# Opening transfers planned with other lengths, new block ranks, and the first 128 keys in one load by ScalarE

## The chip, the cores and the metric

The kernel runs on one core of one Trainium2 chip. The metric is device microseconds of one execution; the kernel before takes 880.31 us (median of 3 runs, 880.14 to 880.77).

## What is computed

Three layers follow one another. First, attention with a sliding window of 64 keys on 4 sequences of 576 tokens, 8 heads of 64:

```python
scores = scale * np.matmul(q, k.transpose(0, 1, 3, 2))
mask = (rel >= 0) & (rel < window)
attn = softmax(np.where(mask, scores, -1e9)); attn_out = np.matmul(attn, v)
```

Its 2304 x 512 result goes through a gated layer (weights 512 x 1536 twice and 1536 x 512) and then through a second one (512 x 2048, 2048 x 512):

```python
xn = x / sqrt(mean(x*x) + 1e-6) * rms_g
y  = (silu(xn @ w_gate) * (xn @ w_val)) @ w_out
h  = y @ w_in;  out = (np.maximum(h, 0) ** 2) @ w_out2
```

Weights arrive as 8-byte numbers and are turned into a high and a low part on the chip ("decode").

## The kernel before

One function lists the work as steps: an engine (or two that may do it), a planned length, the tiles read and written, a rank, and a lag, the planned time from a step's end until its result can be used. `Schedule.issue` then lays all steps out against these planned lengths, always taking on the engine that is free first the step of lowest rank that is ready, and emits the instructions in that order. Each engine runs its own list in that order, and waits where an input is late. The lists are SP (SyncE, which issues nearly all transfers), PE, DVE, ACT, POOL. Where the plan leaves PE without work early on, it puts in matmuls on a constant tile (L1270, "filler").

Attention is cut into 36 blocks of 64 queries, n = 0, 1, 2, ... in the order of the list BLOCK. The order of sequences starts with blocks 0 and 1 of each sequence. For a block: load q (L461), keys (L437) and values (L465); scores on PE (L484); mask and row minimum on DVE (L489); exponentials on ACT (L491); transposes on PE (L500); copy of these by ACT or DVE (L258, tile pt); product with the values on PE (L510); division on DVE (L515); squares on ACT or DVE (L520, L522). Four or six blocks make a tile; per tile a matmul sums the squares (L535), DVE and POOL make the factor (L536, L537), DVE scales (L551), PE transposes (L556), ACT or DVE writes the high part (L258, R<-ps) and DVE the low part (L259, R<-ps).

With a tile's rows and decoded weights the gated layer's products run on PE (L660, L662, L664: "up" with R as input, "down" with ah, al or L). The decode of a pair of weights is: two loads into Q (L591), one scaling by ACT (L605) or DVE (L607), two casts by ACT (L610, L611), two steps by DVE (L612, L613), an addition (L614), then the split into parts (L258 R<-Q, L259 R<-Q). PE's up and down products fill the gaps between attention steps, by rank.

From about 157 us on, five groups of the rest of the first layer run; their upper products (L1116) read quarter sums of the tokens (xq), fetched by SP (L1091) into two slots in turn: a fetch can start when the product two before it has ended. In between SP also writes decoded weights of the second layer to scratch (L768, su and sd). From about 520 us the second layer runs (L883, L959).

Two helpers are named later: `attention(blocks, rank)` and `rms(t, rank, part)` make the steps above with a rank from `rank_at`, to which the lists BLOCK_RANK and NORM_RANK add an offset each.

Of the kernel before, what the change touches and what calls it, by code (L numbers as in the profile page):

```python
# [9 lines left out]
F32 = mybir.dt.float32  # L10
# [33 lines left out]
KW = 4  # L44
GROUPS = [2, 2, 2, 2, 2]
W0 = 9
QTILE, QRANK = 4, 68.0
BLOCK_RANK = [-9.1, 12.7, 56.1, -1.2, -48.4, -18.4, -13.1, -3.7, -7.9, 5.6, 2.2, 2.0, 3.1, 4.8, 3.7, -10.1, 1.4, 2.5, -2.8, -5.7]
NORM_RANK = [-15.0, -1.0, 11.2, 13.4, 14.7, 8.7, 2.9, -0.5]
FIRSTW = [-900.0, -14.0, -5.0]  # L50
CUT, VLATE = 1, 2.3
A1, A2 = 4, 4
S1, S2 = 2, 2
ZONE = 2 * UN
# [5 lines left out]
PG = 2  # L60
G32 = 32
SINGLE = 4
LEAD = 22.6
ELEAD = 13.7
FILL = 1.6, 9.0, 0.45
PORT, SHARED, OPENING = 1.0, 1.5, 0.3

# [180 lines left out]
def attn_moe_moe2(ctx: ExitStack, tc: tile.TileContext, qT, kT, vw, w1, w2, w3, w4, rms_g, out):  # L248
# [8 lines left out]
    nc = tc.nc  # L257
# [3 lines left out]
    sc = Schedule()  # L261
# [18 lines left out]
    T = Tiles()  # L280
# [92 lines left out]
    def at(*a, **k):  # L373
        attn_steps.append(sc.add(*a, **k))
# [7 lines left out]
    def setup():  # L382
        def build_mask():
            nc.gpsimd.memset(T["mask"], 0.0)

            for j in range(2):
                m = T["mask"][64 * j : 64 * j + 64, :]
                nc.gpsimd.affine_select(out=m, in_=m, compare_op=ALU.is_gt, fill=NEG, base=0, pattern=[[1, P]], channel_multiplier=-1)
                nc.gpsimd.affine_select(out=m, in_=m, compare_op=ALU.is_ge, fill=NEG, base=64, pattern=[[-1, P]], channel_multiplier=1)

        def build_ident():
            nc.gpsimd.memset(T["ident"], 1.0)
            nc.gpsimd.affine_select(out=T["ident"], in_=T["ident"], compare_op=ALU.is_equal, fill=0.0, base=0, pattern=[[-1, P]], channel_multiplier=1)
# [12 lines left out]

        at("pool", 0.3, build_expo, w=["expo"])
        at("pool", 1.0, build_comb, w=["comb"])
        at("act", 0.7, lambda: nc.scalar.dma_start(out=T["g"], in_=rms_g), w=["g"], lag=2.5, rank=-1001.0)
        g0 = NBLK - 4  # L410
        gb = T["acc"][:, :, g0 * WIN : (g0 + 1) * WIN]
        at("dve", 0.33, lambda: nc.vector.tensor_scalar(gb, T["g"].unsqueeze(2).to_broadcast([P, KC, WIN]), DM**0.5, None, op0=ALU.mult), r=["g"], w=allk("acc", (g0, 1)))
        gp = ps[R_BANK].rearrange("p (i r) -> p i r", i=NP)[:, :2]

        def spread_g():

            for h in range(2):
# [9 lines left out]
    def load_keys(b, i, rank):  # L427

        w0, w1 = max(i - 1, 0), KEYS[i]
        off = 2 * (b % 2) if i == 0 else 0  # L430
        k = k_tile[0][0] if off else k_ring.next()
        k_tile[0] = k, off - w0
        cuts = (0, 1, 2) if b == i == 0 else (w0, w1)
        for c0, c1 in zip(cuts, cuts[1:]):
            d = slice((c0 + off - w0) * WIN, (c1 + off - w0) * WIN)
            queue = "act" if b == i == c0 == 0 else "sp"
            at("sp", 0.2 + (c1 - c0) * WIN / 105, lambda c0=c0, c1=c1, d=d, queue=queue: (nc.scalar if queue == "act" else nc.sync).dma_start(out=T[k][:, :, d], in_=kT[b, :, :, c0 * WIN : c1 * WIN]), w=[(k, c) for c in range(c0 + off - w0, c1 + off - w0)], lag=2.0, rank=rank + c0 - 0.6 if i == 0 and b < 2 else None)  # L437

    def attention(blocks, rank):

# [10 lines left out]
    def block(n, rank, part, pos):  # L451

        b, i = BLOCK[n]
        nk = WIN if i == 0 else 2 * WIN
        early = lambda late: rank + late if n < T1[0][1] else None
        q, sm, pt = (r.next() for r in (q_ring, sm_ring, pt_ring))
        if i != 1:
            v_tile[0] = v_ring.next()
        v = v_tile[0]
        nb, su, rs = (small[i].next() for i in ("nb", "sum", "rs"))  # L460
        at("sp", 0.6, lambda: nc.sync.dma_start(out=T[q], in_=qT[b * NB + i]), w=[q], lag=2.0, rank=early(-0.5))  # L461
        if i in KEYS:
            load_keys(b, i, rank)
        if i != 1:
            at("sp", 0.75, lambda: nc.sync.dma_start(out=T[v], in_=vw[b * NB + i]), w=[v], lag=2.0, rank=early(VLATE))  # L465
        k, k0 = k_tile[0]
        k0 = (max(i - 1, 0) + k0) * WIN
        keys_ = T[k][:, :, k0 : k0 + nk]
# [108 lines left out]
    closed, closed2 = [], []  # L577
    early = iter(FIRSTW)

    def decode(srcs, rank=None, after=()):  # L580

        n = len(srcs) * WE
# [5 lines left out]
            raws, da, df = [f"raw{h}"], f"da{h}", f"{df_ring.slots[0]}{h}"  # L588
            raw = raws[0]
        for z, src in zip(raws, srcs):  # L590
            sc.add("sp", 2.4 if closed2 else 1.5, lambda z=z, src=src: nc.sync.dma_start(out=T[z], in_=src), w=[z], lag=2.2, rank=rank, after=after)  # L591
        part = lambda i: T[raw].rearrange("p (a b) -> p a b", b=2)[:, :, i]
        a = lambda: T[da]
        f = lambda: T[df]
# [163 lines left out]
    def park(src, keys_, n, dst, key):  # L758

        g = stage_ring.next()  # L760
        v = lambda i=slice(0, 2): T[g][:, : 2 * n].rearrange("p (h n) -> p h n", h=2)[:, i]

        def like(x):
            return x.rearrange("p (i m) -> p i m", m=256) if len(src().shape) == 3 else x

        sc.add(AD, c_ad(n), lambda e: copy(e, like(v(0)), src()), r=keys_, w=[g], port=True)
        sc.add(DP, c_dp(n), lambda e: two(e, like(v(1)), src(), like(v(0)).bitcast(F32), ALU.subtract), r=keys_ + [g], w=[g], port=True)
        sc.add("sp", 0.8 if n == 256 else 1.6, lambda: nc.sync.dma_start(out=dst, in_=v().bitcast(F32)), r=[g], w=[key], lag=2.5)  # L768

    def park_pair(z, p, srcs, swap):  # L770
        f = decode(srcs, after=closed2)
# [246 lines left out]
    QUADS = (B11, B21, R2, R3, R4, R1, B22)  # L1018
# [158 lines left out]
    n = 0  # L1177
    while n < NBLK:
        k = FIRST[max(i for i, t in enumerate(T1) if t[0] <= n)]
# [3 lines left out]
        n = e  # L1183
# [12 lines left out]
    todo, n = [], 0  # L1196
# [317 lines left out]
```

## Time and profile before

| | us |
|---|---|
| median of 3 runs | 880.31 |
| profiled execution | 879.84 |
| its span, first to last instruction | 878.1 |
| PE busy | 866.8 |
| DVE busy | 713.4 |
| ACT busy | 585.3 |

A row of the timeline gives the start, the length, the engine, the line, what is written <- read, and how many instructions it merges; in brackets stands the idle time of the engine before it and what ended it. A window's row gives the busy time and count of each engine, the granted TensorE clock and the share of the transfer engines. "PE" is the matmuls, "PEld" the weight loads beside them; one matmul of the program on 128 x 128 fp32 tiles with a constant as input is recorded as two.

### The profile page before, as it was taken

The page shows a single profiled execution, that of the slowest core. Times are in us where ns is not written, and L with a number is a line of the kernel's source. Part 1 is how long each engine was busy: PE and PEld are TensorE (multiplying, and loading weights), DVE is VectorE, ACT ScalarE, POOL GpSimd, SP SyncE. Part 2 cuts the span into 40 slices and gives each one's busy share as a digit, 9 for nine tenths or more (in the row PEclk, how much of TensorE's full clock was granted, in tenths as well). Part 3 has the DMA queues.
Part 4 walks back from the last instruction along what each step waited for, and adds up shares of the span by engine and source line. Part 5 has one row for each costly group of instructions (what it writes and reads, how often), then busy time and mean ns, then how long its engine had stood idle before and what let it go on. Part 6 is the DMA issues. An engine that isn't in the chain of part 4 may idle for free.

```text
span 878.1 us, 15620 instructions
## 1 busy us (share of the span) xinstructions
PE 866.8 (99%) x5766; PEld 810.5 (92%) x5766; DVE 713.4 (81%) x1407; ACT 585.3 (67%) x1194; POOL 129.3 (15%) x139
## 2 busy tenths in 40 slices
PE   8999999999999999999999999999999999999998
PEld 6789999989889889879989889999999999999997
DVE  5899997887897888898898877678885788767695
ACT  6999885666796786777677676546645546565360
POOL 4545550000040030040022000000100002000010
PEclk9999999999999999999999999999999999999999
DMA  8696782277777968768778698887779776788762
GB/s 262 198 293 220 253 301 89 97 276 253 263 288 267 322 225 299 265 241 299 256 262 266 227 311 293 302 295 264 249 261 305 265 252 238 259 289 290 254 205 72
DMA packets 88059, 222.26 MB, mean 253 GB/s; under 512 B 8240, under 2 KB 30256, under 8 KB 83504
## 3 DMA queue, kind: packets, MB, share of 16 engines
q1 hardware_dynamic: 86304, 220.46, 72.8%
q10 hardware_dynamic: 1680, 0.82, 0.3%
q8 instruction: 45, 0.74, 0.3%
q14 instruction: 30, 0.25, 0.1%
HBM read 179.83 MB, written 41.42 MB: 252 GB/s over the span
## 4 chain that ended last, share of the span: by engine, by line
PE 88%; DVE 6%; ACT 4%; issue 1%; DMA 0%; ACTq 0%; DVEq 0%
PE ps L883 20%; PE ps L959 19%; PE ps L660 12%; PE ps L662 11%; PE ps L664 11%; PE ps L1116 11%; ACT sm L491 2%; PE ps L484 1%; PE ps L500 1%; PE ps L510 1%; DVE sm L489 1%; ACT acc L491 1%; DVE R L259 1%; DVE Q L260 1%; DVE R L260 1%
## 5 line engine op out<-in xcount | busy, mean ns | idle before, releaser
L883 PE MATMUL ps<-R 128*128 128x384 f32 x1008 | 180.6, 334 | 0.0
L883 PEld LDWEIGHTS ps<-R 128*128 128x128 f32 x1008 | 175.4, 188 | 0.3
L959 PE MATMUL ps<-R,L 128*128 128x384 f32 x462 | 155.0, 336 | 0.0
L258 ACT COPY acc<-ps 128x384 f32<-128x384 f32 (+2 forms) x131 | 65.4, 501 | 57.5 <-PE ps L664 29.9
L1116 PE MATMUL ps<-R 128*128 128x512 f32 x420 | 101.8, 390 | 0.0
L1116 PEld LDWEIGHTS ps<-R 128*128 128x128 f32 x420 | 78.7, 188 | 15.8
L967 DVE TENSOR_TENSOR acc<-ps,acc 128x384 f32<-128x384 f32 x101 | 55.4, 555 | 40.9 <-PE ps L959 40.9
L959 PEld LDWEIGHTS ps<-R,L 128*128 128x128 f32 x462 | 86.6, 187 | 0.0
L660 PE MATMUL ps<-R 128*128 128x384 f32 (+2 forms) x368 | 79.9, 339 | 0.6 <-DVE s L713 0.6
L662 PE MATMUL ps<-R 128*128 128x384 f32 (+2 forms) x368 | 78.0, 333 | 0.0
L664 PE MATMUL ps<-R 128*128 128x384 f32 (+2 forms) x368 | 77.8, 333 | 0.0
L959 PE MATMUL ps<-L,R 128*128 128x384 f32 x220 | 74.1, 337 | 0.2 <-DVE acc L967 0.2
L660 PEld LDWEIGHTS ps<-R 128*128 128x128 f32 x368 | 61.9, 189 | 5.5 <-DVE s L713 0.9
L662 PEld LDWEIGHTS ps<-R 128*128 128x128 f32 x368 | 62.4, 188 | 3.2
L664 PEld LDWEIGHTS ps<-R 128*128 128x128 f32 x368 | 62.2, 189 | 3.2
L660 PE MATMUL ps<-L,R 128*128 128x512 f32 (+1 forms) x200 | 57.5, 368 | 0.5 <-ACT ps L742 0.5
L742 ACT COPY ps<-acc 128x512 f32<-128x512 f32 (+1 forms) x97 | 52.8, 554 | 7.7 <-DVE acc L258 5.4
L258 ACT CAST L<-Q 128x512 fp32r<-128x512 f32 (+2 forms) x80 | 44.1, 559 | 20.1 <-DVE Q L710 11.5
L662 PE MATMUL ps<-L,R 128*128 128x512 f32 (+1 forms) x200 | 57.4, 368 | 0.0
L664 PE MATMUL ps<-L,R 128*128 128x512 f32 (+1 forms) x200 | 57.4, 368 | 0.0
L931 ACT CAST L<-Q 128x1152 fp32r<-128x1152 f32 (+1 forms) x22 | 22.0, 998 | 50.1 <-PE ps L959 44.9
L959 PE MATMUL ps<-X,R 128*128 128x384 f32 x154 | 51.1, 332 | 0.0
(153 smaller groups left out, 1826.2 us busy)
## 6 DMA issues: line engine op xcount, KB each, us to landing
R<-xq SPq DMA_DIRECT2D x35, 1024.0 KB, 6.0
Q<-w SPq DMA_DIRECT2D x68, 512.0 KB, 4.7
R<-su SPq DMA_DIRECT2D x24, 1024.0 KB, 5.9
R<-su SPq DMA_DIRECT2D x24, 768.0 KB, 6.1
R<-sd SPq DMA_DIRECT2D x13, 1024.0 KB, 5.7
su<-L SPq DMA_DIRECT2D x24, 512.0 KB, 3.8
sd<-L SPq DMA_DIRECT2D x24, 512.0 KB, 5.2
L<-sd SPq DMA_DIRECT2D x11, 1024.0 KB, 7.7
```

Of the source, the lines that this page charges most:

```text
L258: copy = lambda e, out, in_: nc.scalar.copy(out, in_) if e == "act" else nc.vector.tensor_copy(out, in_)
L260: two = lambda e, out, a, b, op: (nc.vector if e == "dve" else nc.gpsimd).tensor_tensor(out, a, b, op=op)
L491: at("act", 0.37, lambda p=p: nc.scalar.activation(T[sm][:, p, :nk], T[sm][:, p, :nk], AF.Exp, bias=T[nb][:, p : p + 1], scale=-1.0, accum ...
L660: nc.tensor.matmul(acc, wh, xh, start=(i == 0 and not seeded), stop=False, skip_group_check=seeded)
L662: nc.tensor.matmul(acc, wl, xh, start=False, stop=False, skip_group_check=seeded)
L664: nc.tensor.matmul(acc, wh, xl, start=False, stop=(i == n - 1), skip_group_check=seeded)
L742: add("act", c_act(n), lambda b=b, dst=dst: nc.scalar.copy(ps[b][:, :n], dst), r=keys("acc", c, t), w=[("ps", b)])
L883: nc.tensor.matmul(bank, w_, x_, start=(start and i == 0), stop=(i == len(terms) - 1), skip_group_check=True)
L931: sc.add("act", c_act(m * PN), lambda z=z, o=o, m=m: nc.scalar.copy(z("h"), e(o, m)), r=ek(o, m), w=bk("h"))
L959: nc.tensor.matmul(bank, w_, x_, start=(start and i == 0), stop=(i == len(terms) - 1), skip_group_check=True)
L967: sc.add("dve", c_dve(PN), lambda: nc.vector.tensor_tensor(y(i, j), src, y(i, j), op=ALU.add), r=[key], w=yk(i, j), urgent=rush)
L1116: nc.tensor.matmul(ps[bank], w_, x_, start=(start and n == 0), stop=(n == len(terms) - 1), skip_group_check=True)
```

## The change

The first 128 keys of sequence 0 came in two loads of 64, one issued by ACT and one by SP; now one load of 128 is issued by ACT. The values of block 0 move from SP to ACT, and rms_g from ACT to SP. The planned lengths and lags of loads and stores change, by which the planner orders everything. The offsets of ranks change for all blocks and tiles, as does the tile after which the quarter sums are made (QTILE). The diff, without the lists:

```diff
-QTILE, QRANK = 4, 68.0
+QTILE, QRANK = 5, 129.0
-FIRSTW = [-900.0, -14.0, -5.0]
-CUT, VLATE = 1, 2.3
+FIRSTW = [-800.0, -5.0, -5.0]
+CUT, VLATE = 0, 1.3
-LEAD = 22.6
-ELEAD = 13.7
+LEAD = 28.7
+ELEAD = 15.9
-BLOCK_RANK = [-9.1, 12.7, 56.1, ...
+BLOCK_RANK = [-1.8, 4.2, 90.5, ...
...
-        at("act", 0.7, lambda: nc.scalar.dma_start(out=T["g"], in_=rms_g), w=["g"], lag=2.5, rank=-1001.0)
+        at("sp", 0.42, lambda: nc.sync.dma_start(out=T["g"], in_=rms_g), w=["g"], lag=2.5, rank=-1000.0)
...
-        cuts = (0, 1, 2) if b == i == 0 else (w0, w1)
-        for c0, c1 in zip(cuts, cuts[1:]):
...
+        c0, c1 = w0, w1
+        queue = "act" if b == i == 0 else "sp"
+        at(queue, 0.63 if queue == "act" else 0.05 + (c1 - c0) * WIN / 200, ... lag=2.5, ...)
...
-        at("sp", 0.6, lambda: nc.sync.dma_start(out=T[q], in_=qT[b * NB + i]), w=[q], lag=2.0, rank=early(-0.5))
+        at("sp", 0.42, lambda: nc.sync.dma_start(out=T[q], in_=qT[b * NB + i]), w=[q], lag=2.2, rank=early(-0.5))
...
+            queue, dma = ("act", nc.scalar) if n == 0 else ("sp", nc.sync)
+            at(queue, 0.65, lambda: dma.dma_start(out=T[v], in_=vw[b * NB + i]), w=[v], lag=2.3, rank=early(VLATE))
...
-  sc.add("sp", 2.4 if closed2 else 1.5, ...   # weight load, L591
+  sc.add("sp", 2.4 if closed2 else 1.4, ...
-  ... lag=2.5)                                # store to su, sd, L768
+  ... lag=2.2)
-  ... lag=3.5)                                # fetch of xq, L1091
+  ... lag=2.2)
```

How the instructions stand. First SP's list at the start of the program, before (q_97, q_98, q_99 are three slots for queries, k_100 and k_101 two for keys, v_102 to v_105 four for values, Q the raw weights):

```order
L461 DMA q_97<-qT 128x256
L437 DMA k_100<-kT 128x4x64
L465 DMA v_102<-vw 128x512
L461 DMA q_98<-qT 128x256
L437 DMA k_100<-kT 128x4x128
L461 DMA q_97<-qT 128x256
L461 DMA q_99<-qT 128x256
L465 DMA v_103<-vw 128x512
L591 DMA Q<-w 128x1024 x2
```

and now, where ACT's list opens with the load of k_100 (128x4x128) and of v_102:

```order
L460 DMA q_97<-qT 128x256
L409 DMA g<-rms_g 128x4
L460 DMA q_98<-qT 128x256
L436 DMA k_100<-kT 128x4x128
L460 DMA q_99<-qT 128x256
L465 DMA v_103<-vw 128x512
L591 DMA Q<-w 128x1024
L460 DMA q_97<-qT 128x256
L591 DMA Q<-w 128x1024
```

Queries of blocks 1 and 2 and the first weight load stand further ahead; the second weight load now stands behind the second load into q_97, which waits until block 0's scores have read that slot.

Second, ACT's list around the scaling of the second pair of weights (L605), before (nb_89 to nb_92 and sum_115 to sum_118 are slots of blocks in turn, ps_65 and ps_67 hold the first tile's transposed rows):

```order
L491 ACTIVATE acc,sum_117<-acc,nb_91 128x64 x2
L258 CAST R<-ps_67 128x4x128
L491 ACTIVATE acc,sum_117<-acc,nb_91 128x64 x2
L491 ACTIVATE sm_106,sum_118<-sm_106,nb_92 128x128 x3
L258 CAST R<-ps_65 128x4x128
L258 COPY pt_108<-ps_70 64x512
L491 ACTIVATE sm_106,sum_118<-sm_106,nb_92 128x128
L605 ACTIVATE Q<-Q 128x1024
```

and now:

```order
L520 ACTIVATE R,part_124<-acc 128x4x64
L605 ACTIVATE Q<-Q 128x1024
L491 ACTIVATE acc,sum_117<-acc,nb_91 128x64 x4
L491 ACTIVATE sm_106,sum_118<-sm_106,nb_92 128x128 x4
L610 ACTIVATE Q<-Q 128x1024
L520 ACTIVATE R,part_125<-acc 128x4x64
L258 CAST R<-ps_67 128x4x128
```

The scaling moved ahead of eight exponentials and of the cast of the first tile's rows; the cast from ps_65 left ACT's list for DVE's.

Third, PE's list in the first group of upper products, at the fourth product's second half (ps_68) and the fifth product (ps_67, ps_68), before:

```order
L1116 MATMUL ps_68<-R 128x512 x6
L660 MATMUL ps_66<-R 128x512 x4
L662 MATMUL ps_66<-R 128x512 x4
L664 MATMUL ps_66<-R 128x512 x4
L1116 MATMUL ps_67<-R 128x512 x6
L1116 MATMUL ps_68<-R 128x512 x6
```

and now:

```order
L1116 MATMUL ps_68<-R 128x512 x6
L1116 MATMUL ps_67<-R 128x512 x6
L660 MATMUL ps_71<-L,R 128x384 x2
L662 MATMUL ps_71<-L,R 128x384 x2
L664 MATMUL ps_71<-L,R 128x384 x2
L1116 MATMUL ps_68<-R 128x512 x6
```

Two up products of 512 columns that stood between the fourth and the sixth product (the second one further down) now stand behind the sixth. The order of all engines in the last third of the program is the same as before.

## Rows read from the trace of the kernel before

**Rows 1.** The page: busy us of each engine, its share, instructions.

```profile
PE 866.8 (99%) x5766; PEld 810.5 (92%) x5766; DVE 713.4 (81%) x1407; ACT 585.3 (67%) x1194; POOL 129.3 (15%) x139
```

**Rows 2.** Windows: stretch, its length, busy us by engine, clock, DMA.

```profile
0.00:30.00 30.00, 24.89 (x349) 20.37 (x350) 18.84 (x97) 22.14 (x85) 13.87 (x34) 1.00 0.81 251
30.00:50.00 20.00, 18.72 (x281) 16.06 (x279) 18.05 (x72) 19.94 (x70) 10.10 (x14) 1.00 0.72 233
50.00:140.00 90.00, 89.81 (x1235) 83.41 (x1228) 86.19 (x330) 79.30 (x284) 43.31 (x50) 1.00 0.78 257
140.00:520.00 380.00, 379.51 (x1887) 339.22 (x1886) 324.79 (x523) 275.13 (x442) 46.93 (x35) 1.00 0.72 250
```

**Rows 3.** The first window again, PE's fillers (L1270) alone.

```profile
0.00:30.00 30.00, 7.34 (x40) 6.28 (x40) 1.00 0.81 251
```

**Rows 4.** Timeline of the first 8 us: first loads, first scores.

```profile
0.78 0.42 ACTq L409 DMA_DIRECT2D g<-rms_g  x1
...
1.23 0.63 ACTq L437 DMA_DIRECT2D k<-kT  x1
...
4.64 0.71 PE L484 MATMUL ps<-k,q 64*64 64x64 f32 x16 [0.73 <-DMA k<-kT]
...
5.28 1.13 PE L419 MATMUL ps<-ident,acc 128*64 128x128 f32 x8
...
6.33 1.13 PE L484 MATMUL ps<-k,q 64*64 64x128 f32 x16
...
7.51 0.29 DVE L489 CUSTOM_DVE_ANT_0 sm<-ps,mask 128x128 f32<-128x128 f32 x1 [1.34 <-PE ps L484]
```

**Rows 5.** Key loads issued in 0 to 2 us: two of 64.

```profile
DMA to landing us min/median/max: 3.3/3.4/3.5
```

**Rows 6.** Key load issued at 3.13 us: one of 128.

```profile
DMA to landing us min/median/max: 3.6/3.6/3.6
```

**Rows 7.** Weight loads issued at 19.4 and 19.8 us (tile Q).

```profile
DMA to landing us min/median/max: 4.4/4.8/5.2
```

**Rows 8.** Timeline, DVE and SP, 9 to 30 us: copy, decode, scaling.

```profile
9.08 0.68 DVE L258 COPY pt<-ps 64x512 f32<-64x512 f32 x1 [0.63 <-PE ps L500]
...
13.04 0.68 DVE L607 TENSOR_SCALAR Q<-Q 128x1024 f32<-128x1024 f32 x1
...
17.77 1.23 DVE L614 CUSTOM_DVE_ANT_0 Q<-Q 128x2048 uint16<-128x2048 uint16 x1 [0.92 <-ACT Q L611]
...
19.37 0.84 SPq L591 DMA_DIRECT2D Q<-w  x2
...
23.60 0.88 DVE L551 SCALAR_TENSOR_TENSOR xw<-acc,r,gg 128x256 f32<-128x256 f32 x2 [1.31 <-POOL r L537]
...
28.62 0.69 DVE L259 TENSOR_TENSOR R<-ps,R 128x512 fp32r<-128x512 f32 x1
...
29.36 1.16 ACT L605 ACTIVATE Q<-Q 128x1024 f32<-128x1024 f32 x1
```

**Rows 9.** Timeline of PE, 29 to 40 us: first up product, products, transposes.

```profile
29.61 0.72 PE L660 MATMUL ps<-R 128*128 128x256 f32 x4
...
31.20 1.30 PE L510 MATMUL ps<-v,pt 64*64 64x64 f32 x32
32.43 0.66 PE L500 MATMUL ps<-ident,sm 128*128 128x128 f32 x4
...
38.20 1.10 PE L500 MATMUL ps<-ident,sm 128*128 128x128 f32 x3 [0.22 <-ACT sm L491]
```

**Rows 10.** PE at the fourth, fifth and sixth upper product.

```profile
211.35 1.55 PE L1116 MATMUL ps<-R 128*128 128x512 f32 x6
...
215.47 2.88 PE L1116 MATMUL ps<-R 128*128 128x512 f32 x12
...
225.17 2.92 PE L1116 MATMUL ps<-R 128*128 128x512 f32 x12
```

**Rows 11.** The 33 fetches of xq from 160 to 520 us.

```profile
DMA to landing us min/median/max: 4.6/6.0/8.4
```

More of the change, by code (lines that the diff above doesn't have):

```diff
@@ L46 @@
 W0 = 9
-QTILE, QRANK = 4, 68.0
-BLOCK_RANK = [-9.1, 12.7, 56.1, -1.2, -48.4, -18.4, -13.1, -3.7, -7.9, 5.6, 2.2, 2.0, 3.1, 4.8, 3.7, -10.1, 1.4, 2.5, -2.8, -5.7]
-NORM_RANK = [-15.0, -1.0, 11.2, 13.4, 14.7, 8.7, 2.9, -0.5]
-FIRSTW = [-900.0, -14.0, -5.0]
-CUT, VLATE = 1, 2.3
+QTILE, QRANK = 5, 129.0
+BLOCK_RANK = [-1.8, 4.2, 90.5, 37.4, -151.0, -71.5, -55.0, -5.5, -5.0, -0.6, 11.4, 15.1, -2.8, -4.4, -10.5, -13.2, -1.2, -4.0, -1.3, 3.3]
+NORM_RANK = [-104.3, -15.1, 12.3, 17.1, 2.9, -6.5, -5.5, 15.1]
+FIRSTW = [-800.0, -5.0, -5.0]
+CUT, VLATE = 0, 1.3
 A1, A2 = 4, 4
@@ L432, in load_keys @@
         k_tile[0] = k, off - w0
-        cuts = (0, 1, 2) if b == i == 0 else (w0, w1)
-        for c0, c1 in zip(cuts, cuts[1:]):
-            d = slice((c0 + off - w0) * WIN, (c1 + off - w0) * WIN)
-            queue = "act" if b == i == c0 == 0 else "sp"
-            at("sp", 0.2 + (c1 - c0) * WIN / 105, lambda c0=c0, c1=c1, d=d, queue=queue: (nc.scalar if queue == "act" else nc.sync).dma_start(out=T[k][:, :, d], in_=kT[b, :, :, c0 * WIN : c1 * WIN]), w=[(k, c) for c in range(c0 + off - w0, c1 + off - w0)], lag=2.0, rank=rank + c0 - 0.6 if i == 0 and b < 2 else None)
+        c0, c1 = w0, w1
+        d = slice(off * WIN, (c1 + off - w0) * WIN)
+        queue = "act" if b == i == 0 else "sp"
+        at(queue, 0.63 if queue == "act" else 0.05 + (c1 - c0) * WIN / 200, lambda: (nc.scalar if queue == "act" else nc.sync).dma_start(out=T[k][:, :, d], in_=kT[b, :, :, c0 * WIN : c1 * WIN]), w=[(k, c) for c in range(c0 + off - w0, c1 + off - w0)], lag=2.5, rank=rank + c0 - 0.6 if i == 0 and b < 2 else None)
     def attention(blocks, rank):
@@ L464, in block @@
         if i != 1:
-            at("sp", 0.75, lambda: nc.sync.dma_start(out=T[v], in_=vw[b * NB + i]), w=[v], lag=2.0, rank=early(VLATE))
+            queue, dma = ("act", nc.scalar) if n == 0 else ("sp", nc.sync)
+            at(queue, 0.65, lambda: dma.dma_start(out=T[v], in_=vw[b * NB + i]), w=[v], lag=2.3, rank=early(VLATE))
         k, k0 = k_tile[0]
@@ L590, in decode @@
         for z, src in zip(raws, srcs):
-            sc.add("sp", 2.4 if closed2 else 1.5, lambda z=z, src=src: nc.sync.dma_start(out=T[z], in_=src), w=[z], lag=2.2, rank=rank, after=after)
+            sc.add("sp", 2.4 if closed2 else 1.4, lambda z=z, src=src: nc.sync.dma_start(out=T[z], in_=src), w=[z], lag=2.2, rank=rank, after=after)
         part = lambda i: T[raw].rearrange("p (a b) -> p a b", b=2)[:, :, i]
@@ L767, in park @@
         sc.add(DP, c_dp(n), lambda e: two(e, like(v(1)), src(), like(v(0)).bitcast(F32), ALU.subtract), r=keys_ + [g], w=[g], port=True)
-        sc.add("sp", 0.8 if n == 256 else 1.6, lambda: nc.sync.dma_start(out=dst, in_=v().bitcast(F32)), r=[g], w=[key], lag=2.5)
+        sc.add("sp", 0.8 if n == 256 else 1.6, lambda: nc.sync.dma_start(out=dst, in_=v().bitcast(F32)), r=[g], w=[key], lag=2.2)
     def park_pair(z, p, srcs, swap):
@@ L1090, in fetch @@
         x = xr_ring.next()
-        sc.add("sp", 3.4, lambda: nc.sync.dma_start(out=T[x].bitcast(F32), in_=T["xq"][QUADS[m]].rearrange("p z n -> p (z n)")), r=[("xq", QUADS[m], z) for z in range(2)], w=[x], lag=3.5)
+        sc.add("sp", 3.4, lambda: nc.sync.dma_start(out=T[x].bitcast(F32), in_=T["xq"][QUADS[m]].rearrange("p z n -> p (z n)")), r=[("xq", QUADS[m], z) for z in range(2)], w=[x], lag=2.2)
         return x
```

## The prediction, made before the changed kernel ran

> **What bounds the kernel now.** I read the page first. PE is busy 99% of the span, DVE 81% and ACT 67% [rows 1]. The share is an average, so the windows by stage come next [rows 2]. From 140 to 520 us PE is idle for 0.49 us of 380, and from 50 to 140 us for 0.19 of 90. All that PE can still be given lies ahead of 50 us: 5.11 us idle in the first 30, of which filler matmuls take another 7.34 [rows 3], and 1.28 us from 30 to 50 us. In the first 30 us DVE (18.84) and ACT (22.14) are not full either: they wait for transfers and for each other. From 30 us on ACT is full (19.94 of 20) and from 50 us DVE nearly (86.19 of 90). The real matmuls are the same in both kernels (PE's list loses two fillers of 20), and after the opening PE runs through. So the change moves the end by as much as PE gains or loses up to about 50 us, plus new holes in the stage after, where SP's and PE's lists changed too.
>
> **The head.** ACT used to issue rms_g at 0.78 us and the keys at 1.23; the first scores wait for these keys and start at 4.64 [rows 4]. Now the keys are ACT's first load, 0.45 us earlier. The load has twice the bytes. A load of 64 keys took 3.3 to 3.5 us [rows 5], one of 128 took 3.6 [rows 6]; that one had other loads beside it, as this one has. With 3.0 as my estimate, somewhat below both since fewer bytes are in flight ahead of it, the scores start at about 3.9 instead of 4.64: 0.7 us. The ends are 3.6 (0.2 us gained) and 2.0, an estimate with twice the rate of 128 keys (1.8 us gained).
>
> The Trainium skill (DMA: Bandwidth & Descriptors, "Issuing engines are not separate DMA queues") says that loads from ScalarE and SyncE share the same transfer engines, and that a second issuer saves only the issue time. By that, moving the first values to ACT would give nothing but SP's slot, and the head would gain just the 0.45 us; the equal lengths in rows 5 and 6 cannot decide it. The sum below does not use this.
>
> The second block's scores came at 6.33, behind the four rms_g matmuls of L419 (1.13 us by their row); these now stand behind them, and DVE's wait of 1.34 us before the second block's minima goes [rows 4]. Take 1.0 us.
>
> **The first up product.** PE wastes time until up products can start, at 29.61 [rows 9]. In the row before it DVE's last step for it, the low part of the first tile, ran from 28.62 to 29.31 [rows 8]. Up to there DVE had worked about 18.3 us (18.84 in 30 us, less some 0.5 that lies behind that step) and idled 11.0. In the new list more stands ahead of the same step: three more copies of transposed blocks and one cast, 4 x 0.68; two more decode steps, 2 x 0.68; six more row minima, 6 x 0.29; one sum of squares less, about 0.4. That is 5.4 by their lengths, and about 5.0 as neighbours overlap a little on the engine: 23.3 us of work. The idle time becomes 11.0 less 0.7 (head), less 1.0 (second block), less 1.3 (the wait for POOL at 23.60 [rows 8], which two decode steps and other minima now fill), and less 1.2 for the first weights: L607 started at 13.04, its two loads now stand seventh and ninth in SP's list instead of ninth and tenth, but the second waits for block 0's scores, and the loads ahead of them share the way. That would be 6.8.
>
> Against this stands L605, the scaling of the second pair of weights. ACT began it at 29.36; now it stands ahead of eight exponentials and of the cast that the first up product needs. About 5.9 us of ACT's work is no longer ahead of it, so ACT, which also gains a good half microsecond early, reaches it at about 22. Its loads were issued at 19.37 and took up to 5.2 us, the second landing near 25.0 [rows 7, 8]. They wait for ACT's L611 before, and now stand ahead of one value load, so I put the landing at 23.5; bounds 21.4 (issue right behind an earlier L611) and 25.0 (as before). ACT then stands still for 1.5 us (0 to 3.0), and everything behind it waits: the exponentials of two blocks, the cast, and DVE behind the cast. Idle 8.3 and work 23.3 put the first up product at 31.6; the ends are 30.1 and 33.1.
>
> That is 2.0 us later than 29.61. But PE has done the two blocks' value products by then (16 instructions, 1.30 us by the row of the same size at 31.20 [rows 9]; the 16 there are recorded as 32). So PE falls back 0.7 us (from 0.8 ahead to 2.2 back).
>
> **What is given back.** At this point DVE is ahead by 5.0 - 2.0 = 3.0 us of work. From 30 to 50 us PE has 1.28 us idle [rows 2], and matmuls stretched by late operands: three transposes at 38.20 took 1.10, where four took 0.66 at 32.43 [rows 9]; over the stretch I estimate another 1.2 from such rows. Of these 2.5 us the lead should return 1.8; bounds 0 and 2.5. From 50 to 140 us 0.19 us of idle time leaves nothing to gain; a loss there needs a new hole (bound 1.0).
>
> **The stage after.** The planned lag of the xq fetch fell from 3.5 to 2.2. It now puts the first group's fifth product right behind the fourth, and the sixth comes nearer. A fetch can be issued when the fourth ends: at 211.35 + 1.39 = 212.9 before, and the sixth product used it at 225.17, 12.3 us later [rows 10]. Two up products of 512 columns, 12 matmuls each, leave that stretch. The row of 215.47 has 12 of that size at 2.88 us; the last overlaps what follows, so I take 2.7 each, and 6.9 us remain. Fetches landed after 4.6 to 8.4 us, median 6.0 [rows 11]. The median fits, the longest makes PE wait 1.5; I take 0.3. All other fetches keep at least 6.9 as well. The remaining reordering up to 520 us I cost at nothing, since PE's 0.49 us there was hidden before behind the same engines with a fifth of their time free (ACT 275, DVE 325 of 380); bounds -0.3 and +0.8.
>
> **Sum.** 0.7 - 1.8 + 0.3 = -0.8 us, so 879.84 becomes 879.0 for the profiled execution. That execution was 0.47 below the median of the runs, so I predict 880.31 - 0.8 = 879.5.
>
> **Rivals.**
> *The opening gains more.* If the second weights land by the time ACT reaches L605 (21.4 to 22), the first up product starts at 30.1, PE is 0.8 ahead instead of 0.7 back, and DVE's lead of 4.5 closes the whole 2.5 us: -3.3, with 0.3 for the fetch -3.0, so 877.3. For it speaks that every early load stands further ahead in SP's list; against it that the same bytes share the way (0.81 of the transfer engines' time in the first 30 us [rows 2]). Even half of this, 1.8 us, is counted here. Chance 0.36.
> *ACT stands still at L605.* If these weights land at 25.0 as before, ACT waits 3.0, the first up product starts at 33.1, PE is 2.2 back, and the lead of 1.5 returns at most 0.6 of the 2.5, since ACT, which is full from 30 us on, cannot catch up: +1.6, and with the fetch +1.9, so 882.2. It decides from a landing of about 24.8 on. Chance 0.13.
> *The sixth product's fetch is late.* SP issues in order, and two weight loads and two scratch stores stand ahead of that fetch, which wait for the decode. If they hold it for 2 us beyond the 212.9 of before, moved 5.4 earlier, and it takes the 8.4 us, PE waits 3.5: +2.4, so 882.7. Chance 0.05.
> *The change does not reach the chip's head*: the keys land no earlier, since all loads share the way. Then 0.5 of the 0.7 is lost, and 880.0 comes out; this is part of the forecast's own range, 878.6 to 882.0.
>
> **Chances.** A change under 0.2% (1.76 us) cannot be told from none here. Faster by more than that (below 878.55): 0.36, the first rival. Within it: 0.46, the forecast. Slower (over 882.07): 0.18, the next two. The range of 8 in 10 goes from 876.8 (the first rival at its better half) to 882.2.
>
> **What would show it.** Right: first scores near 3.9 us; the second block's scores before L419; ACT idle before L605 for 1 to 2 us; the first L660 at 31 to 32; PE's idle time from 30 to 50 us below 0.6; from 50 us on the same windows. The step on L605 is wrong if ACT has no wait there; the step on the lead if PE idles over 1.2 us from 30 to 50. A wait of L1116 for R<-xq near 220 us would show the third rival. The forecast as a whole is wrong if the end differs by more than 1.76 us from 880.31.

## The result, and the profile after

The change made the kernel slower: 887.14 us median (886.08 to 887.65) against 880.31 (879.91 to 880.78) in the same rounds, a ratio of 1.0076 with a 95% interval of 1.0064 to 1.0087. Forecast were 879.5, with 882.2 as the upper end. The profiled execution has a span of 885.9 us, 7.8 more than before.

First the windows by stage, which answer to [rows 2]. Columns: the stretch, its length, then busy us and instructions of PE, PEld, DVE, ACT and POOL, the granted clock, DMA share, GB/s.

```profile
0.00:30.00 30.00, 24.59 (x335) 19.42 (x336) 19.13 (x92) 22.07 (x83) 16.55 (x34) 1.00 0.80 254
30.00:50.00 20.00, 19.21 (x288) 16.53 (x287) 19.72 (x86) 19.21 (x67) 11.09 (x14) 1.00 0.62 195
50.00:140.00 90.00, 85.92 (x1196) 78.34 (x1195) 82.97 (x320) 79.33 (x285) 42.94 (x51) 1.00 0.80 265
140.00:520.00 380.00, 378.59 (x1884) 339.28 (x1883) 320.59 (x509) 270.05 (x437) 49.67 (x39) 1.00 0.68 244
```

PE's idle time went from 5.11 to 5.41 us up to 30, from 1.28 to 0.79 up to 50, from 0.19 to **4.08** between 50 and 140, and from 0.49 to 1.41 up to 520. The loss begins where the prediction saw nothing to lose.

The first large hole, a stretch in which PE stands idle, lies at 60 to 65 us. The timeline of after, with what released an engine in brackets:

```profile
53.24 0.47 SPq L591 DMA_DIRECT2D Q<-w  x1
...
61.38 1.15 ACT L605 ACTIVATE Q<-Q 128x1024 f32<-128x1024 f32 x1 [1.72 <-DMA Q<-w]
...
62.96 0.33 PE L500 MATMUL ps<-ident,sm 128*128 128x128 f32 x1 [0.68 <-ACT sm L491]
...
63.40 0.69 DVE L259 TENSOR_TENSOR R<-ps,R 128x512 fp32r<-128x512 f32 x1 [0.89 <-ACT R L258]
...
63.82 0.33 PE L500 MATMUL ps<-ident,sm 128*128 128x128 f32 x1 [0.53 <-ACT sm L491]
```

The second half of the fourth pair of weights was issued at 53.24, landed 8.0 us later and was used 0.1 us after that. ACT reached its scaling L605 too early and stood still for 1.72 us, with the exponentials behind it in its list; PE's transposes L500 waited for these. In before this pair landed no earlier: its second half was issued at 54.6 us and took 7.1. But there the scaling was DVE's (L607), which came to it with no wait, behind row minima:

```profile
62.01 0.68 DVE L607 TENSOR_SCALAR Q<-Q 128x1024 f32<-128x1024 f32 x1
```

Of the first six scalings ACT has three in before and five in after. So it is not a late landing that is new at this hole, but which engine comes to it how early, and what stands behind that instruction. The second hole, 75 us later, begins in the same way:

```profile
126.13 0.33 SPq L591 DMA_DIRECT2D Q<-w  x1
...
131.62 1.15 ACT L605 ACTIVATE Q<-Q 128x1024 f32<-128x1024 f32 x1 [1.68 <-DMA Q<-w]
...
132.81 0.69 DVE L612 TENSOR_SCALAR Q<-Q 128x1024 f32<-128x1024 f32 x1 [2.45 <-ACT Q L605]
...
137.11 1.22 DVE L614 CUSTOM_DVE_ANT_0 Q<-Q 128x2048 uint16<-128x2048 uint16 x1
138.25 0.42 DVE L259 TENSOR_TENSOR al<-s,ah 128x256 fp32r<-128x256 f32 x1
138.59 0.41 DVE L713 SCALAR_TENSOR_TENSOR s<-s,ps 128x256 f32<-128x256 f32 x1
...
139.06 0.51 PE L660 MATMUL ps<-ah,R 128*128 128x256 f32 x2 [1.71 <-DVE s L713]
```

The late decode pushes its step L614 in front of the short steps that PE waits for, and PE idles 1.71 us. Then a second price comes, in the clock (windows of after, columns as above):

```profile
136.00:138.00 2.00, 1.35 (x11) 1.14 (x9) 1.86 (x4) 1.12 (x4) 0.00 (x0) 1.00 0.95 373
138.00:140.00 2.00, 0.94 (x8) 0.94 (x9) 1.50 (x6) 1.29 (x3) 0.32 (x1) 1.00 0.90 334
140.00:142.00 2.00, 2.00 (x12) 2.00 (x11) 1.30 (x3) 1.09 (x3) 1.00 (x1) 0.50 0.06 23
142.00:144.00 2.00, 2.00 (x10) 2.00 (x10) 1.43 (x4) 0.70 (x1) 0.00 (x0) 0.65 0.00 0
144.00:146.00 2.00, 2.00 (x17) 1.96 (x16) 1.97 (x5) 0.82 (x2) 0.00 (x0) 1.00 0.00 0
```

After four microseconds in which PE was busy for 2.29, the granted clock was 0.50, the lower of its two levels (1.2 of 2.4 GHz), and was back at 1.00 from 144 us on: 2 x 0.50 + 2 x 0.35 = 1.7 us of matmul time lost while PE counts as fully busy.

So of the 7.8 us of span, 3.9 are new idle time between 50 and 140, 1.7 the clock behind it, 0.9 new idle time up to 520 (a wait of 1.4 us of L660 for ACT's L742 near 390, which was 0.5 before), and 1.3 remain that no row names. PE's busy time is 3.7 us longer than before (870.5 against 866.8) for the same products, 1.7 of it by the clock; matmuls stretched by late operands are the likely rest, which is not shown. Up to 50 us the kernels are level: PE's busy time less fillers is 36.3 us in before and 36.4 in after.

The head answers to [rows 4]:

```profile
0.79 0.64 ACTq L436 DMA_DIRECT2D k<-kT  x1
...
4.28 0.70 PE L484 MATMUL ps<-k,q 64*64 64x64 f32 x16 [0.79 <-DMA k<-kT]
...
5.95 1.13 PE L484 MATMUL ps<-k,q 64*64 64x128 f32 x16 [0.96 <-DMA q<-qT]
7.01 1.13 PE L419 MATMUL ps<-ident,acc 128*64 128x128 f32 x8
...
7.25 0.23 DVE L489 CUSTOM_DVE_ANT_0 acc<-ps,mask 128x64 f32<-128x64 f32 x1 [2.76 <-PE ps L484]
```

The scores start 0.36 us earlier, close to the 0.44 by which the keys were issued earlier. The Trainium skill (DMA: Bandwidth & Descriptors, "Issuing engines are not separate DMA queues") allows just the issue time for such a move; the trace agrees. But DVE's first minima start at 7.25 instead of 5.50, though the first block's scores were done by 5.0. The two blocks' scores are halves of the same PSUM tiles, and the second block's now stand ahead of the first block's minima in the recorded program: the minima wait for both (minfirst below shows it). The second block's minima start at 7.83 instead of 7.51.

### The profile page after: what moved, and what is told of

It reads as the page before. It is cut to its first block, busy times and chain, and to the rows that moved or that the text cites. A ratio compares the mean times of both kernels' runs of the same rounds, so it can differ in the third digit from the quotient of the medians.

```text
span 885.9 us, 15623 instructions
## 1 busy us (share of the span) xinstructions
PE 870.5 (98%) x5762; PEld 812.4 (92%) x5762; DVE 715.6 (81%) x1401; ACT 584.4 (66%) x1196; POOL 135.3 (15%) x142
## 4 chain that ended last, share of the span: by engine, by line
PE 87%; DVE 6%; ACT 2%; DMA 2%; issue 1%; POOL 1%; SPq 0%; DVEq 0%; ACTq 0%; POOLq 0%
PE ps L883 20%; PE ps L959 19%; PE ps L660 11%; PE ps L662 11%; PE ps L664 11%; PE ps L1116 11%; PE ps L510 1%; PE ps L500 1%; PE ps L484 1%; DMA Q<-w 1%; DMA q<-qT 1%; ACT sm L491 1%; DVE R L259 1%; DVE Q L614 1%; DVE sm L489 1%
## 5 line engine op out<-in xcount | busy, mean ns | idle before, releaser
L1116 PE MATMUL ps<-R 128*128 128x512 f32 x420 | 102.1, 390 | 0.0
L258 ACT COPY acc<-ps 128x384 f32<-128x384 f32 (+2 forms) x128 | 62.9, 495 | 53.5 <-PE ps L959 26.7
L1116 PEld LDWEIGHTS ps<-R 128*128 128x128 f32 x420 | 78.6, 188 | 15.7
L660 PE MATMUL ps<-R 128*128 128x384 f32 (+2 forms) x368 | 80.3, 340 | 0.0
L660 PEld LDWEIGHTS ps<-R 128*128 128x128 f32 x368 | 62.6, 190 | 4.9 <-issue 0.9
L258 ACT CAST L<-Q 128x512 fp32r<-128x512 f32 (+2 forms) x86 | 48.9, 576 | 21.2 <-DVE Q L710 13.0
L742 ACT COPY ps<-acc 128x512 f32<-128x512 f32 (+1 forms) x97 | 52.9, 555 | 12.2 <-DVE acc L258 10.5
L660 PE MATMUL ps<-L,R 128*128 128x512 f32 (+1 forms) x200 | 57.6, 369 | 1.4 <-ACT ps L742 1.4
```

The lines of the kernel that those rows point to most:

```text
L258: copy = lambda e, out, in_: nc.scalar.copy(out, in_) if e == "act" else nc.vector.tensor_copy(out, in_)
L660: nc.tensor.matmul(acc, wh, xh, start=(i == 0 and not seeded), stop=False, skip_group_check=seeded)
L742: add("act", c_act(n), lambda b=b, dst=dst: nc.scalar.copy(ps[b][:, :n], dst), r=keys("acc", c, t), w=[("ps", b)])
L1116: nc.tensor.matmul(ps[bank], w_, x_, start=(start and n == 0), stop=(n == len(terms) - 1), skip_group_check=True)
```

## The experiments

Ratios are to the kernel before, run on the same chip in the same rounds. For the experiments that move single instructions, the planner's picks are first collected and recorded only after a rearrangement, so that all else stays as planned:

```diff
-            fn(e)
+            emitted.append((i, fn, (e,)))
 ...
+        for i, fn, args in rearrange(emitted):
+            fn(*args)
```

Line numbers in their profiles are higher by 14 (minfirst, l605late, l614late), 18 (headloads) or 20 (beforefill); L484 of after is L498 there.

**minfirst: the head's wait alone.** Steps 12 to 15 are the first block's minima, 27 the second block's scores. The order on every engine is that of after.

```diff
+    emitted = move(emitted, [12, 13, 14, 15], before=27)
```

> The kernel after, with every engine's order of instructions unchanged; only the program records the first block's four row minima ahead of the second block's scores, so that they no longer wait for those scores. Theory H (the 6.8 us come from the head: DVE's and ACT's start is 1.75 us late, and the holes at 60 to 65 and at 135 to 140 us follow from it): first minima near 5.1 instead of 7.25 us, first up product about 31.0 instead of 32.7, both holes gone or halved, time 880.5 to 883. Theory L (the holes come from where the decode steps of the weights stand in ACT's and DVE's lists, whatever the head does): first minima near 5.1 as well, but ACT still stands 1 us or more at L605 near 61 us and PE still idles over 1 us near 138 us, time 885.5 to 887.

Measured: 886.56 us (883.84 to 889.43), ratio 1.0070 (1.0052 to 1.0088). The wait is gone, the gain is not there (timeline):

```profile
5.08 0.23 DVE L503 CUSTOM_DVE_ANT_0 acc<-ps,mask 128x64 f32<-128x64 f32 x1 [0.56 <-PE ps L498]
...
8.76 1.06 PE L514 MATMUL ps<-ident,acc 128*64 128x128 f32 x4
...
17.42 1.06 PE L514 MATMUL ps<-ident,sm 128*64 128x128 f32 x4
...
32.78 0.74 PE L674 MATMUL ps<-R 128*128 128x256 f32 x4
```

The minima start 2.2 us earlier, and the first up product comes at 32.78, as in after (32.69). ACT still waits 3.8 us for weights, and the time lies where theory L had it; theory H falls. The same hole before 140 us was left here, but this time the clock stayed up (windows):

```profile
136.00:138.00 2.00, 1.16 (x9) 0.95 (x8) 1.86 (x3) 0.99 (x4) 0.00 (x0) 1.00 0.98 399
138.00:140.00 2.00, 1.13 (x9) 1.13 (x10) 1.50 (x6) 1.42 (x4) 0.51 (x1) 1.00 0.86 305
140.00:142.00 2.00, 2.00 (x17) 2.00 (x16) 1.39 (x5) 0.91 (x3) 0.81 (x1) 1.00 0.11 45
```

The fall of the clock is thus not certain behind such a hole. The two profiled executions are 1.70 us apart (885.95 and 887.65), just what the rows give for the clock. In the five runs of after, three with a mean granted clock of 0.997 or 0.998 took 887.1 to 887.7, two with 0.999 or 1.000 took 886.1 and 886.6. The Trainium skill (TensorE: Matmul & The Clock Gate, "The HAM clock gate") says that the point at which the clock rises varies between runs of one kernel. In this pair of traces, with the same order on every engine, it is a fall that came in one execution and not in the other.

**l605late: the first hole.** Step 201 is the scaling L605 of 61.38 us; 438 is the last exponential of the block that PE waits for.

```diff
+    emitted = move(emitted, [201], behind=438)
```

> The kernel after, with one instruction moved: ACT's scaling L605 of the third weights, for which it stood still 1.72 us until 61.38, comes three ACT instructions later. Theory L: ACT's wait there goes, PE's idle time from 60 to 70 us falls from 1.61 to below 0.5, time 885.7 to 886.3 (1.2 us gained, at most 0.4 given back later). Theory H, and the rival that DVE's work is what bounds this stage: PE's hole only moves to a later place and the time stays at 886.8 to 887.4.

Measured: 885.05 us (883.82 to 885.98), ratio 1.0049 (1.0037 to 1.0061): 2 us less than after.

```profile
60.00:70.00 10.00, 9.50 (x124) 8.74 (x124) 9.26 (x42) 9.86 (x30) 2.93 (x4) 1.00 0.88 310
130.00:140.00 10.00, 8.29 (x69) 7.87 (x66) 7.03 (x17) 7.03 (x13) 1.32 (x1) 1.00 0.68 248
140.00:145.00 5.00, 5.00 (x37) 4.96 (x35) 4.97 (x11) 3.15 (x6) 0.00 (x0) 1.00 0.01 3
```

PE's idle time there fell from 1.61 to 0.50, and the later hole is untouched. The gain is not given back; the rival falls. It is larger than the 1.2 expected, and the time lies below the expected range; the mean granted clock was 0.999 or 1.0 in these five runs, and 1.00 behind the later hole in the profiled one, so some of it is the clock.

**l614late: the second hole.** Steps 950 and 952 are L614 and the cast behind it, 757 the second low part al.

```diff
+    emitted = move(emitted, [950, 952], behind=757)
```

> The kernel after, with two instructions moved: DVE's L614 at 137.1 us and the ACT cast that needs it come behind the two tiles' L713, L714, the cast ah and the low part al, for which PE waited 1.71 us until 139.06; all other orders are unchanged. Theory L with the clock: PE's idle time from 135 to 140 us falls from 1.71 to about 0.3, the granted clock from 140 to 145 us stays at 1.00 instead of 0.66, and the time falls by 1.4 for the idle time and 1.7 for the stretch at half clock: 883.6 to 884.6. Rival without the clock (the slower matmuls there had another cause, or the later weights cost as much): 885.4 to 886.4.

Measured: 886.21 us (884.28 to 887.45), ratio 1.0059 (1.0047 to 1.0071).

```profile
60.00:70.00 10.00, 6.31 (x62) 5.54 (x64) 5.89 (x19) 6.73 (x23) 2.96 (x4) 1.00 0.78 289
130.00:140.00 10.00, 10.00 (x109) 9.80 (x108) 7.98 (x23) 7.63 (x16) 0.71 (x1) 1.00 0.89 336
140.00:145.00 5.00, 5.00 (x39) 4.96 (x38) 4.96 (x11) 3.80 (x8) 0.61 (x1) 1.00 0.14 56
```

The second hole is gone and the clock stays at 1.00, as theory L has it; the time lies in the rival's range. In this execution the weights of the first hole landed later still, since SP issued the second half at 54.78 instead of 53.24 and it took 8.4 us instead of 8.0 (timeline):

```profile
63.27 1.12 ACT L619 ACTIVATE Q<-Q 128x1024 f32<-128x1024 f32 x1 [3.83 <-DMA Q<-w]
```

PE's hole there was 3.69 us instead of 1.61, so the time tells little: a list whose stall hangs on one transfer's landing has no steady price. The runs spread over 3.2 us.

**all3: the three edits together.**

> The kernel after with the three edits together: minima of the first block recorded ahead of the second block's scores, L605 of the third weights three ACT instructions later, L614 of the fifth weights behind the low part al. Theory L: the gains of the single edits add up to within 0.7 us, time about 881.5 to 883.5. Theory H: the same time as the first edit alone gives.

Measured: 882.96 us (881.71 to 886.2), ratio 1.0030 (1.0020 to 1.0040). Over 4 of the 6.8 us come back, and the three single gains (0.6, 2.1 and 0.9) add up to 3.6; theory L holds, H does not. The 2.6 us that are left over before have not been traced to their causes one by one. The profiled execution shows 1.1 us more idle time than before from 50 to 140 us and 0.9 more from 380 to 400. Its clock fell too, but much earlier, and what that cost the end is not shown (windows):

```profile
30.00:32.00 2.00, 1.59 (x19) 1.47 (x20) 2.00 (x13) 2.00 (x5) 0.00 (x0) 0.64 0.00 0
32.00:34.00 2.00, 2.00 (x11) 2.00 (x11) 2.00 (x11) 2.00 (x12) 1.11 (x2) 0.51 0.72 203
```

**headloads: the new loads in the old order.** On before, the first 128 keys in one load as ACT's first issue, the first values as ACT's second, rms_g second on SP; nothing else moves.

```diff
-        at("act", 0.7, lambda: nc.scalar.dma_start(out=T["g"], in_=rms_g), ...
+        at("act", 0.7, lambda: nc.sync.dma_start(out=T["g"], in_=rms_g), ...
+            if b == i == 0:
+                load = (lambda: nc.scalar.dma_start(out=T[k][:, :, : 2 * WIN], ...)) if c0 == 0 else lambda: None
 ...
-            at("sp", 0.75, lambda: nc.sync.dma_start(out=T[v], ...
+            at("sp", 0.75, lambda: (nc.scalar if n == 0 else nc.sync).dma_start(out=T[v], ...
+    emitted = move(emitted, [4], behind=8)
```

> The kernel before, with the new loads of the head alone: the first 128 keys in one load as ACT's first issue, the first values as ACT's second, rms_g second on SP; every other instruction in the order of before. Theory L (the loads are harmless, the loss lies in the order of the instructions): first scores near 4.3 instead of 4.64 us, no new hole behind 50 us, time 879.7 to 880.6. Rival (the loads themselves cost, by what they delay): a hole or a wait for a load in the first 60 us that before does not have, time 881.5 or more.

Measured: 879.22 us (878.21 to 879.81) against 880.43, ratio 0.9982 (0.9973 to 0.9991). It is the only version faster than both kernels, by a little more than expected. Timeline, PE:

```profile
4.19 0.70 PE L502 MATMUL ps<-k,q 64*64 64x64 f32 x16 [0.27 <-DMA k<-kT]
...
6.99 0.60 PE L518 MATMUL ps<-ident,acc 128*64 128x128 f32 x4
...
28.11 0.72 PE L678 MATMUL ps<-R 128*128 128x256 f32 x4
```

The first up product comes 1.5 us earlier than in before [rows 9], and 1.2 us reach the end. So the visible part of the change is a gain; the loss lies in the new order.

**oldlags, oldranks, oldlens, klen, beforeklen, wlag: what in the planner makes it.** Each undoes or does one part of the planner's numbers and lets it plan anew, so each is another order throughout, and its time is that of one plan. Only oldlags leaves the order of after in place up to about 110 us.

```
oldlags (on after)       - xq, su, sd: lag=2.2
                         + xq: lag=3.5; su, sd: lag=2.5
oldranks (on after)      QTILE, QRANK, BLOCK_RANK, NORM_RANK, FIRSTW, VLATE, LEAD, ELEAD of before
oldlens (on after)       - q 0.42, v 0.65, k 0.05 + (c1 - c0) * WIN / 200, w 1.4
                         + q 0.6, v 0.75, k 0.2 + (c1 - c0) * WIN / 105, w 1.5; lag=2.0 for q, k, v
klen (on after)          - k 0.05 + (c1 - c0) * WIN / 200
                         + k 0.2 + (c1 - c0) * WIN / 105
beforeklen (on before)   the same line the other way round
wlag (on after)          - weights of the opening: lag=2.2
                         + weights of the opening: lag=5.0
```

> The kernel after with the planned lags of the xq fetches and of the stores of su and sd as in before (3.5 and 2.5 for 2.2); the order up to about 110 us is that of after on every engine. Theory L: the holes ahead of 145 us stay, PE's idle time from 380 to 400 us falls from 1.07 to about 0.5, time 885.8 to 886.8. Rival (the new lags cost more than that hole, by matmuls stretched between 140 and 520 us): time below 885.5. Rival (the new lags are a gain): above 887.4.

> The kernel after, loads and planned lengths as they are, but all ranks and leads of before (block, norm, first weights, quads, LEAD, ELEAD, VLATE), so that the planner lays the opening out anew. If the ranks chosen for after are what costs: at least one of the two holes (60 to 65, 135 to 140 us) is gone, time 880 to 884. If the planned lengths and lags of the transfers cost, whatever the ranks: ACT waits over 1 us for weights at L605 at some place between 40 and 140 us and the time is 885 or more.

> The kernel after with the planned lengths and lags of before for the loads of queries, values, keys and weights (0.6, 0.75, 0.2 + columns / 105 and 1.5 for 0.42, 0.65, 0.05 + columns / 200 and 1.4); the loads of the head and all new ranks stay, and the planner lays the opening out anew. Theory P (the shorter planned lengths let the plan issue loads faster than the chip moves them, so that ACT meets weights that have not landed): ACT waits less than 0.5 us in sum for weights at L605 between 40 and 140 us, time 879 to 883. Rival (the new ranks cost, whatever the lengths): holes of 1 us or more between 45 and 140 us, time 884 or more.

> The kernel after with the planned length of the key loads alone as in before (256 columns 2.64 instead of 1.33). Theory P, with the keys as the largest change of length: most of the loss is gone, 880 to 884. If the keys' length is not what counts: 885 or more.

> The kernel before with the planned length of the key loads alone as in after (0.05 + columns / 200). Theory P: new waits of ACT for weights at L605 or of PE for loads between 40 and 140 us, time 882 to 886. Rival (the lengths do no harm by themselves): within 1 us of before, 879.5 to 881.4.

> The kernel after with one planned number changed: the weights of the opening count as landed 5.0 us behind their issue instead of 2.2 (the traces show 4.4 to 7.2). The planner then puts L605 later on ACT or the loads earlier on SP. If L605's standing too early in ACT's list is the cause: ACT's wait for weights between 40 and 140 us below 0.5 us, PE's idle time from 60 to 70 us below 0.5 and no hole over 1 us near 138, time 881 to 884. Rival (the plan has other faults that weigh as much): 884.5 or more.

Measured, with PE's idle time from 50 to 140 us and ACT's waits for weights from 30 to 145 us in each one's profiled execution:

| kernel | median us | ratio, interval | PE idle 50:140 | ACT for weights |
|---|---|---|---|---|
| headloads | 879.22 | 0.9982 (0.9973 to 0.9991) | 0.19 | 1.3 |
| beforeklen | 882.52 | 1.0022 (1.0010 to 1.0033) | 0.94 | 2.3 |
| wlag | 882.71 | 1.0033 (1.0021 to 1.0045) | 1.04 | 0 |
| all3 | 882.96 | 1.0030 (1.0020 to 1.0040) | 1.31 | 1.6 |
| klen | 883.57 | 1.0038 (1.0025 to 1.0050) | 1.85 | 2.3 |
| l605late | 885.05 | 1.0049 (1.0037 to 1.0061) | 2.94 | 1.9 |
| oldranks | 885.52 | 1.0054 (1.0042 to 1.0066) | 3.67 | 3.3 |
| oldlags | 886.09 | 1.0068 (1.0055 to 1.0080) | 3.99 | 3.3 |
| l614late | 886.21 | 1.0059 (1.0047 to 1.0071) | 4.43 | 4.2 |
| fill | 886.43 | 1.0065 (1.0053 to 1.0077) | 4.17 | 3.2 |
| oldlens | 886.48 | 1.0067 (1.0054 to 1.0080) | 2.92 | 0.5 |
| minfirst | 886.56 | 1.0070 (1.0052 to 1.0088) | 3.66 | 3.8 |

In before the last two columns read 0.19 and 0, in after 4.08 and 3.4. The median goes roughly with the idle time between 50 and 140 us, whatever was edited; oldlens and l605late, with the same idle time, are 1.4 us apart. ACT's wait need not cost anything: headloads has 1.3 us of it and PE's idle time of before. The idle time leaves out the clock, which also fell in the profiled executions of klen (0.54 and 0.61 from 68 to 72 us) and oldranks (0.70 and 0.50 from 107 to 111 us). Windows of that stretch, in wlag and then in oldlens:

```profile
50.00:140.00 90.00, 88.96 (x1228) 82.55 (x1227) 86.03 (x319) 80.44 (x290) 41.99 (x50) 1.00 0.79 257
```

```profile
50.00:140.00 90.00, 87.08 (x1239) 80.38 (x1240) 85.07 (x315) 81.29 (x305) 44.85 (x53) 1.00 0.82 266
```

One number of the plan, the weights' lag, takes ACT's waits away and brings 4.4 us back (wlag). It is not what the change changed: 2.2 stands in before as well. The old ranks under the new lengths keep the loss (oldranks), and the new length of the keys alone costs before 2.3 us and brings ACT's waits with it (beforeklen, whose runs spread from 880.0 to 884.5). The old length of the keys alone brings 3.6 us back (klen). All these times lie in the ranges expected if the planned lengths are at fault (theory P): the shorter planned lengths let the plan put L605 where the weights have not landed. Then it fails in part: with all old lengths under the new ranks ACT's waits are down to 0.5, but 886.48 is far from the 879 to 883 that P gave. There the loss begins earlier: the first up product came at 33.99 us, and up to 50 us PE's busy time less fillers is 33.8, 2.5 us short of before. Later PE waited 1.7 us for DVE's L259 before L535. Which of the ranks does that, and whether before's ranks and lengths only fit each other, stays open; so does what the choice of ACT instead of DVE for a scaling costs by itself, which no run isolates. The late lags (oldlags) are worth nothing that can be told: the hole at 380 to 400 us goes, and 1.09 us of idle time comes ahead of it.

**fill, beforefill, all3fill: is it PE's speed in the head?** In the head four transposes take longer than later: in after 1.06 us at 9.24, 1.11 at 13.36 and 0.63 at 17.44; in before 1.06 at 7.98 and 0.66 at 11.26; in headloads 0.60 at 6.99 already. The granted clock reads 1.00 in all these stretches, so the rows don't say that this is the clock. Fillers were added in PE's gaps: one ahead of the first scores, two ahead of the second block's, one ahead of the third's (fill, all3fill), or one ahead of the first scores (beforefill).

```
fill (on after), all3fill (on all3)
+    emitted = fill(emitted, 11, 1)
+    emitted = fill(emitted, 27, 2)
+    emitted = fill(emitted, 45, 1)
beforefill (on before)
+    emitted = fill(emitted, 12, 1)
```

The first number is the step ahead of which fillers go (11, 27, 45 and, in before, 12 are the blocks' scores), the second how many.

> The kernel after with four more filler matmuls in PE's list, in the gaps that its trace shows in the head: one ahead of the first scores, two ahead of the second block's, one ahead of the third's. Theory C (in the head PE runs at its lower speed until it has been busy without gaps: four transposes take 1.06 to 1.11 us up to 14 us and 0.63 from 17.4 on, in before 0.66 from 11.3 on): the short durations begin by 12 us, the first up product comes at 31.5 to 32.2 instead of 32.69, the time falls by 0 to 1 us to 886 to 887, since the holes behind 50 us stay. Rival (loads and DVE set the opening): the short durations may begin earlier, the first up product stays at 32.5 or later.

> The kernel before with one more filler matmul ahead of the first scores, in PE's gap of 0.73 us there, and nothing else. With the new loads of the head PE's short durations began at 6 us instead of 11.3, and the first up product came 1.5 us earlier. Theory C (that gain is PE's speed, which rises early when PE has no gap): short durations from about 6 us, first up product 28.2 to 28.9, time 879.0 to 879.9. Rival (the gain is the keys landing earlier): first up product and time as before, 29.4 to 29.8 and 880.2 to 880.6.

> The kernel after with the three repairs and the four fillers together. Theory L with C: what the three repairs left (2.6 us over before) is 0.9 from the hole at 380 to 400 us, which stays, and 1.7 from the opening, of which PE's speed in the head is up to 1: 881.8 to 882.6. Rival (the fillers' gain is eaten again by a fall of the clock behind PE's gaps at 28 to 32 us, as in the run with fillers alone): 882.7 to 883.4.

Measured: fill 886.43 us (ratio in the table), all3fill 882.90 (1.0027, 1.0016 to 1.0038), beforefill 880.77 (1.0000, 0.9992 to 1.0009). The short durations did come early (four transposes took 0.63 us at 9.02 in fill); here PE's timeline in beforefill:

```profile
4.87 0.49 PE L504 MATMUL ps<-k,q 64*64 64x64 f32 x16 [0.53 <-DMA k<-kT]
...
7.17 0.68 PE L520 MATMUL ps<-ident,acc 128*64 128x128 f32 x4
...
29.00 0.72 PE L680 MATMUL ps<-R 128*128 128x256 f32 x4
```

The first up product moved by 0.6 of the 1.5 us of headloads. The span of this execution is 0.7 us shorter than before's (877.4 against 878.1), but the median of the runs is not (880.77 against 880.42). So PE's speed in the head is not shown to have made headloads faster, nor ruled out for a part; the keys that land earlier are the likely cause of the rest, which no run isolates. In fill the gain was eaten before the first up product (at 33.02), where PE waited for DVE and ACT and the granted clock then fell (windows):

```profile
28.00:30.00 2.00, 1.31 (x10) 0.84 (x9) 1.99 (x8) 2.00 (x6) 1.83 (x3) 1.00 0.34 111
30.00:32.00 2.00, 1.35 (x27) 1.05 (x27) 1.75 (x8) 2.00 (x9) 0.29 (x1) 0.90 0.00 0
32.00:34.00 2.00, 2.00 (x19) 1.88 (x17) 2.00 (x11) 2.00 (x6) 0.07 (x1) 0.50 0.20 32
```

The time of all3fill lies in the rival's range, but not for the rival's reason: in its profiled execution the clock stayed at 1.00 from 28 to 36 us, and the first up product came at 31.02, 0.8 earlier than in all3.

## Why the prediction was wrong

**The step that failed** is the term for 50 to 140 us: "0.19 us of idle time leaves nothing to gain; a loss there needs a new hole (bound 1.0)". There were two large holes and some small ones, 3.9 us, and 1.7 of clock behind the second: 5.6 of the 7.8 us of span. The all3 run shows the two large ones as causes (beside minfirst's edit, whose 0.6 us alone is not clear of the noise), and l605late and l614late each by itself in its trace. The bound had been taken from what before idles there; but before's 0.19 us says how well its list fitted the chip, not how little another list can lose. Its DVE was busy 86.19 of 90 us, so a late step in a new list had little to be hidden behind; that this is why no hole was made good is argued, not shown.

**The mechanism had been named, at the wrong place.** The second rival was ACT standing still at L605 with its list behind it, at about 22 us, for +1.9 us and with a chance of 0.13. At 23.87 us ACT had no wait (the falsifier for that step), and none at the third pair (41.4 us); it stood still at the fourth and at the fifth. The prediction weighed L605 once, at the second pair, and did not go through the later pairs in the new order.

**The head, -0.7.** The scores gained 0.36. The 1.0 us of DVE's wait for the second block turned into a wait of 2.76 for both blocks: the prediction looked for what stood ahead of the second block's scores on PE, not for what the minima would wait for. In the end neither mattered: minfirst took the wait away and the first up product stayed.

**The first up product, 31.6.** It came at 32.69. DVE's last step for it ended at 31.41, about where the sum had put it, but by two errors that cancelled: 20.5 us of work instead of 23.3, and 10.9 idle instead of 8.3. PE was still at two blocks' value products (until 32.31) and a filler behind them.

**The lead, -1.8.** From 30 to 50 us PE's idle time fell by 0.49, not by 1.8. At 50 us the kernels were level, where the prediction had after 1.1 ahead.

**The sixth product's fetch, +0.3.** L1116 had no wait for R<-xq; the third rival did not occur. (The fourth product's end, 212.9, is 211.35 + 1.55 by its row; the prediction writes 1.39 there, and its sum is right.) **140 to 520 us:** 0.9 more idle time, just beyond the +0.8 that stood as bound.

The first rival (the opening gains more) is what headloads shows for the loads without the new order, at 1.2 instead of 3.0 us.

## What to carry to other kernels

When a change lets a planner lay out the work anew, a stage that ran without idle time before can lose most, as it did here, and its bound must come from the new order: go through each in-order engine's list and ask, for every transfer it waits on, what stands behind the waiting instruction. Test the visible edit in the old order by itself; here it was a gain of 1.2 us inside a change that lost 6.8. And hold the plan's numbers against the trace: the weights of the opening landed 3.4 to 8.0 us after their issue in after, while the plan gave them 1.4 us of issue and a lag of 2.2. Planning with 5.0 brought back 4.4 us, in the one plan that came of it; before had planned with 2.2 too, and its order hid the late landings.

## What had not been expected of the hardware

A hole's price can be twice its length: PE, busy for 2.29 of 4 us around 138 us, had a granted clock of 0.50 and 0.65 in the next four, which cost 1.7 us more, while the same hole in minfirst (2.29 of 4 as well) left the clock at 1.00. Such a fall of the clock stands in five of the sixteen profiled executions (after, all3, fill, klen, oldranks), leaving aside the last 5 us of each, at places from 30 to 140 us, and costs 1.7 us each time by its rows. And one transfer of 512 KB, at the same place of the same list, was issued between 53.2 and 54.8 us and took 7.4 to 8.4 us to land in four executions of this order (after, minfirst, oldlags, l614late); ACT stood still for it between 1.3 and 3.8 us.
